# Early reads of the weight matrices, a new order of the first matmuls, and a finer last column in a fused GFNet plus gated-MLP kernel

## The chip, the cores and the metric

The kernel runs on one core of one Trainium2 chip. The metric is device time in microseconds (us), the median over several executions. In the text PE is the matmul engine, DVE is VectorE, ACT is ScalarE, POOL is GpSimd, and SP is SyncE, which issues most of the DMAs.

## The reference

x has 2048 rows of 512, in bf16. Three terms are added: x itself, a spectral filter of the normalised x, and a gated MLP of the normalised x.

```python
def reference(A_x, A_w_r, A_w_i, B_x, B_w_gate, B_w_up, B_w_down):
    x = A_x                                   # (1, 2048, 512)
    xn = _layernorm(x, axis=-1)
    # spectral: rfft2(xn) * (w_r + 1j*w_i), then irfft2
    # gated MLP: g = xn @ w_gate, u = xn @ w_up   (512 x 1792)
    #            (gelu(g) * u) @ w_down           (1792 x 512)
    return x + _A_ref(xn, A_w_r, A_w_i) + _B_ref(xn, B_w_gate, B_w_up, B_w_down)
```

## The kernel before

The 2048 rows are 16 "columns" of 128 rows each. A column is loaded, its mean and variance are taken (`stats`, `mean`), it is normalised to `xn`, transposed to `xnT` (columns 0 to 3 on PE, the others by DMA), and multiplied by Wg and Wu into `g_ps` and `u_ps`. Then ACT makes the gelu `ge` and DVE the product `hT`. The spectral part (`bp`, `dp`, `ep`, `gp`, `yp`) is woven between these units. At the end `y_ps` = `hT` times `Wd_sb` is added to x and stored.

A small planner orders all of this. Each operation is entered with an engine, an expected duration, a priority `key`, a landing time `t_min` where it needs a DMA, and the rotating PSUM buffers it takes and gives back. The planner simulates the engines and fixes each engine's order. Nothing is reordered at run time: an engine whose next instruction is not ready simply waits.

```python
    load_x(0, 1)                                   # columns 0 and 1, then weights in thirds
    load_x(1, 1)
    for f0, f1 in ((0, 512), (512, 1024)):
        load_w(Wg_sb, f0, f1)
        load_w(Wu_sb, f0, f1)
        if f0 == 0:
            load_x(2, 2)
    load_x(4, 4)
    # ... the last third of the weights, the rest of x, RF (a DFT table), constants ...
    LAND = {0: 2.9, 1: 3.8, 2: 7.9, 3: 7.9}        # landing times that the planner believes
    WG_LAND = [5.6] * 4 + [9.3] * 4 + [15.0] * 6
    WU_LAND = [7.0] * 4 + [10.8] * 4 + [17.0] * 6
    # ... the index table idx_t, issued last of these ...

def unit(k, c0, n, f0, m=1):                       # n columns, m chunks of 128 features
    g = add("PE", occ, lambda: mm("g_ps", "G", Wg_sb), src, key=1000 + k, acq=("G",), t_min=WG_LAND[f0 + m - 1])
    u = add("PE", occ, lambda: mm("u_ps", "U", Wu_sb), src, key=1000.5 + k, acq=("U",), t_min=WU_LAND[f0 + m - 1])
    # ... ge on ACT, h on DVE ...

todo = [(0, 1, 0, 2), (0, 1, 2, 2), (1, 1, 0, 4), (0, 2, 4, 2), (0, 2, 6, 2)]   # and so on

def forward(cg, kv):                               # bp: first DFT step of four columns
    for q in range(4):
        m = pe(0.224, lambda q=q: mm(q), [f], 10 * cg + q, acq=("S",), ...)
        bs_ops.append(add("ACT", 0.5, lambda q=q: out(q), [m], key=10 + cg + 0.1 * q, rel=("S",)))   # Bs <- bp

def down(c):                                       # y of one column; the last column in two halves
    w = D if c < NC - 1 else D // 2
    for o in range(0, D, w):
        # ... 14 matmuls with Wd, one with RI, the add of x on DVE, the store ...
```

(Cuts are marked with `# ...`; arguments that the argument here does not touch are left out.)

Of the kernel before, what the change touches and what calls it, by code (L numbers as in the profile page):

```python
# [10 lines left out]
P = 128  # L11
# [190 lines left out]
def kernel(  # L202
# [50 lines left out]
    def load_x(c0, n, eng=nc.sync):  # L253
        eng.dma_start(out=x_t[:, c0:c0 + n, :], in_=x_v[:, c0:c0 + n, :])

    def load_w(a, b, eng=nc.sync):
        nc.sync.dma_start(out=Wg_sb[:, :, a:b], in_=wg_v[:, :, a:b])
        eng.dma_start(out=Wu_sb[:, :, a:b], in_=wu_v[:, :, a:b])
# [17 lines left out]

    pin = tc.keep_in_program_order
    pin(nc.scalar.activation(out=root[:], in_=eps_t[:], func=AF.Sqrt, bias=eps_t[:], scale=1.0))
    load_x(0, 1)
    load_x(1, 1)  # L280
    for f0, f1 in ((0, 512), (512, 1024)):
        load_w(Wg_sb, f0, f1)
        load_w(Wu_sb, f0, f1)
        if f0 == 0:
            load_x(2, 2)
    load_x(4, 4)
    load_w(Wg_sb, 1024, DF)
    load_w(Wu_sb, 1024, DF)
    load_x(8, 4)
    nc.sync.dma_start(out=RF_t[:], in_=rf_d.rearrange("p (c k) -> p c k", c=NC))  # L290
    load_x(12, 4)
    load_consts("F0", "M0")
    LAND = {0: 2.9, 1: 3.8, 2: 7.9, 3: 7.9}
    LAND.update({c: 12.6 if c < 8 else 18.5 if c < 12 else 21.5 for c in range(4, NC)})
    WG_LAND = [5.6] * 4 + [9.3] * 4 + [15.0] * 6
    WU_LAND = [7.0] * 4 + [10.8] * 4 + [17.0] * 6
    RF_LAND = 20.0

    idx_t = pc.tile([P, 3], I32, name="idx_t")
    nc.sync.dma_start(out=idx_t[:], in_=nc.inline_tensor(idx_np, name="spec_rows").ap())  # L300
    for T, w_in in ((TR, A_w_r), (TI, A_w_i)):
        rows = w_in.rearrange("(kb a h g) k -> h kb a (g k)", kb=NC, h=2, a=8)
        Tf = T.rearrange("p j k -> p (j k)")
# [76 lines left out]
    def first_two():  # L380
        o = {}

        def v(k, fn, occ, deps=(), lat=None, t_min=0.0):
            o[k] = add("DVE", occ, fn, [o[d] for d in deps], key=-2000 + len(o), lat=lat, t_min=t_min,
                       after=o.get("last"))
            o["last"] = o[k]

        def root_of(c):
            o["root", c] = add("ACT", 0.31, lambda: A.activation(
                out=rstd[:, c:c + 1], in_=mv[:, c, 1:2], func=AF.Sqrt, bias=eps_t[:], scale=1.0),  # L390
                [o["mean", c]], key=-2000 + c)

        def T(c, h):
            o["T", c, h] = add("PE", 0.12, lambda: f_T(c, 2 * h, 2), [o["xn", c, h]], key=-2000 + 2 * c + h,
                               lat=0.36, acq=("S",))

        def recip(c):
            v(("rstd", c), lambda: V.reciprocal(out=rstd[:, c:c + 1], in_=rstd[:, c:c + 1]), 0.15, [("root", c)])

        def xn_(c, h):  # L400
            v(("xn", c, h), lambda: f_norm_v(c, 256 * h, 256), 0.27, [("rstd", c)], lat=0.4)

        def copy(c, h):
            v(("copy", c, h), lambda: f_Tc(c, 2 * h, 2), 0.25, [("T", c, h)], lat=0.4)
            o["copy", c, h].rel = ("S",)

        def stats(c):
            v(("stats", c), lambda: f_stats(c), 0.6, t_min=LAND[c], lat=0.7)

        def mean(c):  # L410
            v(("mean", c), lambda: f_mean(c), 0.1, [("stats", c)])
            root_of(c)

        stats(0)
        mean(0)
        stats(1)
        mean(1)
        recip(0)
        xn_(0, 0)
        xn_(0, 1)  # L420
        recip(1)
        table = add("ACT", 1.3, lambda: None, [o["root", 1]], key=-1500, lat=1.3)
        T(0, 0)
        T(0, 1)
        add("PE", 0.65, spin_on, [o["T", 0, 1]], key=-1500, lat=0.65, after=o["T", 0, 1])
        copy(0, 0)
        copy(0, 1)
        v("xn1", lambda: f_norm_v(1, 0, D), 0.33, [("rstd", 1)], lat=0.45)
        t = add("PE", 0.23, lambda: f_T(1, 0, NE), [o["xn1"]], key=-1998, lat=0.45, acq=("S",))
        xT_op[0], xn_op[0] = o["copy", 0, 1], o["xn", 0, 1]  # L430
        xT_op[1] = add("ACT", 0.5, lambda: f_Tc(1, 0, NE, A.copy), [t, table], key=-1200, rel=("S",))
        xn_op[1] = o["xn1"]
# [3 lines left out]
    def moments(c, key):  # L436
        s = add("DVE", 0.6, lambda: f_stats(c), key=key, t_min=LAND[c] if c < 4 else max(LAND[c], 14.7))
        return add("DVE", 0.1, lambda: f_mean(c), [s], key=key - 0.5)

    def second_two():  # L440
        m = [moments(c, -1200 + c) for c in (2, 3)]
        steps = rsqrt_steps(V, 2, 2)
        m = [add("DVE", 1.5, lambda: [f() for f in steps], m, key=-1190)]
        for c in (2, 3):
            xn_op[c] = add("DVE", 0.33, lambda c=c: f_norm_v(c, 0, D), m, key=-1180 + c, lat=0.53)
            t = add("PE", 0.23, lambda c=c: f_T(c, 0, NE), [xn_op[c]], key=-880 + c, lat=0.5, acq=("S",))
            e, f = ("ACT", A.copy) if c == 2 else ("DVE", V.tensor_copy)
            xT_op[c] = add(e, 0.5, lambda c=c, f=f: f_Tc(c, 0, NE, f), [t], key=-1100 + c, rel=("S",))
# [27 lines left out]
    def unit(k, c0, n, f0, m=1):  # L476
        sb, o, w = c0 // 4, (c0 % 4) * P, n * P
        alloc = None
        if sb < 3 and f0 == 0 and c0 % 4 == 0:
            def alloc():  # L480
                t = pc.tile([P, NFC, 512], BF16, name=f"hT{sb}", tag=("hT0", "hT1", "xn")[sb])
                hT.update({(sb, f): (t, f) for f in range(NFC)})
        elif sb == 3 and f0 % 4 == 0:
            def alloc():
                h = min(4, NFC - f0)
                t = pc.tile([P, h, 512], BF16, name=f"hT3{f0}", tag=("xnT0", "xnT1", "xnT2", "hT3")[f0 // 4])
                hT.update({(sb, f0 + f): (t, f) for f in range(h)})
        b = {}
        rhs = xnT[sb][:, :, c0 % 4:c0 % 4 + n, :].rearrange("p e c q -> p e (c q)")

        def mm(name, tag, W_):
            b[name] = ps.tile([P, m, w], F32, name=name, tag=tag, bufs=2)
            for f in range(m):
                for e in range(NE):
                    T_.matmul(b[name][:, f], lhsT=W_[:, e, (f0 + f) * P:(f0 + f + 1) * P], rhs=rhs[:, e, :],  # L495
                              start=(e == 0), stop=(e == NE - 1))

        def f_ge():
            b["ge"] = pw.tile([P, m, w], BF16, name="ge", bufs=3)
            A.activation(out=b["ge"][:], in_=b["g_ps"][:], func=AF.Gelu_apprx_tanh)  # L500

        def f_h():
            if alloc:
                alloc()
            V.tensor_tensor(out=hT_of(sb, f0, m, o, w), in0=b["u_ps"][:], in1=b["ge"][:], op=ALU.mult)  # L505

        occ = m * {1: 0.228, 2: 0.437, 4: 0.863}[n]
        src = [xT_op[c] for c in range(c0, c0 + n)]
        g = add("PE", occ, lambda: mm("g_ps", "G", Wg_sb), src, key=1000 + k, lat=occ + 0.3, acq=("G",),
                t_min=WG_LAND[f0 + m - 1])  # L510
        u = add("PE", occ, lambda: mm("u_ps", "U", Wu_sb), src, key=1000.5 + k, lat=occ + 0.3, acq=("U",),
                t_min=WU_LAND[f0 + m - 1])
        ge = add("ACT", {1: 0.28, 2: 0.36, 4: 0.5}[n * m], f_ge, [g], key=-1000 + k,
                 lat={1: 0.38, 2: 0.48, 4: 0.7}[n * m], acq=("ge",), rel=("G",))
        h = add("DVE", {1: 0.21, 2: 0.34, 4: 0.61}[n * m], f_h, [ge, u], key=-1000 + k, rel=("U", "ge"))
        for c in range(c0, c0 + n):
            for f in range(f0, f0 + m):
                h_op[c, f] = h

    todo = [(0, 1, 0, 2), (0, 1, 2, 2), (1, 1, 0, 4), (0, 2, 4, 2), (0, 2, 6, 2)]  # L520
    todo += [(2, 2, f, 2) for f in range(0, 8, 2)]
    todo += [(0, 4, f) for f in range(8, NFC)]
    todo += [(4 * sb, 4, f) for sb in range(1, NSB) for f in range(NFC)]
# [269 lines left out]
    def down(c):  # L793
# [20 lines left out]
            nc.sync.dma_start(out=out_v[:, c, o:o + w], in_=b["y"][:, o:o + w])  # L814

        x = add("SP", 0.36, load, key=1000 + c, lat=2.6, acq=("y_sb",), t_min=100.0)
        w = D if c < NC - 1 else D // 2
        for o in range(0, D, w):
            k = 2000 + 10 * c + o / D
            m = add("PE", 14 * w * 0.000421, lambda o=o: mm(o, w), [h_op[c, f] for f in range(NFC)] + [wd],  # L820
                    key=k, acq=("S",))
            r = add("PE", w * 0.000421, lambda o=o: ri_mm(o, w), [m, yt_op[c], ri], key=k + 0.1,
                    lat=w * 0.000421 + 0.3)
            m.lat = m.occ
            t = add("DVE", 0.1 + w * 0.001, lambda o=o: total(o, w), [r, x], key=k, rel=("S",))
            add("SP", 0.36, lambda o=o: store(o, w), [t], key=k, lat=2.0, rel=("y_sb",) if o + w == D else ())

    for c in range(NC):
        down(c)
# [35 lines left out]
```

## Time and profile before

| | before |
|---|---|
| median, four runs | 180.45 us (180.31 to 180.52) |
| span in the profile | 178.5 us |
| PE dense from | about 10.3 us |
| end of the last matmul | 175.13 us |

The first lines are from the page of the kernel before: the span, the busy time and share of each engine with its instruction count (PEld is PE's weight load, which overlaps PE), and the shares of the chain of waits that ended last.

```profile
span 178.5 us, 3086 instructions
...
PE 172.8 (97%) x1100; PEld 95.7 (54%) x1118; DVE 117.0 (66%) x261; ACT 95.9 (54%) x172; POOL 19.6 (11%) x60
...
PE 90%; DMA 4%; ACT 2%; SPq 1%; issue 1%; DVE 1%
...
```

PE is busy 97% of the span, so there seems to be nothing left. The Trainium skill (Perfetto Trace Analysis, "Identifying the Most-Contended Engine") warns that the matmul busy share is a poor measure of headroom. Part of the busy time here is filler (`spin` matmuls that keep PE running while data arrives), so the start has to be read in time.

The timeline of the kernel before, cut to the lines that matter: start in us, duration, engine, source line, operation, output<-inputs, shape, count, and in brackets the idle time before it and what ended it. A merged line's duration includes the modelled end of the last matmul, so read the starts. SPq is SP issuing a DMA.

```profile
1.71 0.43 SPq L275 DMA_DIRECT2D Wg_sb<-in_B_w_gate_dram  x1
...
6.78 0.61 PE L495 MATMUL g_ps<-xnT,Wg_sb 128*128 128x128 bf16 x8
...
8.10 1.07 PE L495 MATMUL u_ps<-xnT,Wu_sb 128*128 128x128 bf16 x16
...
8.76 1.29 DVE L333 BATCH_NORM_STATS2 stats<-x_t 128x6 f32<-128x512 bf16 x2 [2.04 <-DMA x_t<-in_A_x_dram]
...
9.00 1.06 PE L495 MATMUL g_ps<-xnT,Wg_sb 128*128 128x128 bf16 x16
...
10.27 1.05 PE L495 MATMUL g_ps<-xnT,Wg_sb 128*128 128x256 bf16 x8 [0.21 <-DMA Wg_sb<-in_B_w_gate_dram]
...
11.15 1.06 PE L495 MATMUL u_ps<-xnT,Wu_sb 128*128 128x128 bf16 x16
...
22.14 1.03 PE L495 MATMUL g_ps<-xnT,Wg_sb 128*128 128x512 bf16 x3
...
```

Read it from the starts. The first eight g matmuls of column 0 start at 6.78. The u matmuls start at 8.10, when the first piece of Wu lands. Sixteen g matmuls of column 1 start at 9.00 and, at 54 ns each, are done near 9.87. Then PE stands for 0.4 us until 10.27, because its next instruction needs the second piece of Wg. At 11.15 follow sixteen u matmuls of column 1 whose data had been there by 9.0 (Wu from 8.1, column 1's `xnT` at the latest with the g matmuls of 9.00): they could have filled that gap. From 10.27 on PE never waits until well past 22.14, where the wide (512-column) units begin. That start at 22.14 is a good milestone: it holds everything that happened before it.

A table of windows of the same kernel, here for the DMA rate (the last number, in GB/s):

```profile
core 0: us, PE busy (x) PEld busy (x) DVE busy (x) ACT busy (x) POOL busy (x), PEclk, DMA share, GB/s
3.00:3.50 0.50, 0.50 (x5) 0.31 (x3) 0.50 (x1) 0.00 (x0) 0.00 (x0) 1.00 0.47 47
3.50:4.00 0.50, 0.50 (x2) 0.15 (x1) 0.34 (x2) 0.09 (x1) 0.00 (x0) 1.00 0.83 205
4.00:4.50 0.50, 0.50 (x3) 0.21 (x2) 0.48 (x1) 0.20 (x1) 0.00 (x0) 1.00 0.86 285
```

Between 3 and 4 us the DMA engines move little (47, then 205 GB/s). Column 0 of x has landed (its stats start at 2.96), column 1 lands by 4.02, and the first of the weights is only starting. Later the rate is near 390.

Two more places in the PE timeline of the kernel before, near 40 us and at the first dp matmul:

```profile
39.47 1.42 PE L565 MATMUL bp<-RF_t,xf 128*128 128x128 bf16 x16
...
40.73 1.03 PE L495 MATMUL g_ps<-xnT,Wg_sb 128*128 128x512 bf16 x4
...
55.43 0.61 PE L623 MATMUL dp<-CT,Bs 128*128 128x128 bf16 x8
```

Sixteen bp matmuls normally take 0.89 us from start to the next start; here it is 40.73 - 39.47 = 1.26, so 0.37 us are lost. The end of the timeline:

```profile
174.86 0.27 PE L808 MATMUL y_ps<-yt,RI_t 128*128 128x256 bf16 x1
175.17 0.42 DVE L811 TENSOR_TENSOR y_sb<-y_ps,y_sb 128x256 bf16<-128x256 f32 x1 [0.73 <-PE y_ps L808]
```

After that add the last store is issued; its landing takes 1.6 us, and the span ends at 178.5.

### The profile page before, as it was taken

The numbers are of one execution on the slowest core, as the hardware profiler recorded it, in microseconds if no ns is written. First come the engines' busy times: TensorE is split into PE (matmuls) and PEld (weight loads), VectorE is DVE, ScalarE is ACT, GpSimd is POOL, SyncE is SP. The second block draws the span as 40 slices with busy tenths as digits, with TensorE's granted clock in tenths as the row PEclk, the third lists the DMA queues.
The fourth block names the chain that finished last, engine by engine and source line by source line (L and its number), as shares of the span: only waits on it lengthen the run. The fifth ranks groups of instructions, "written<-read, shape, count | busy, mean of one in ns | idle before, by whom it ended". The sixth has DMA issues, their size and how long they took to land.

```text
span 178.5 us, 3086 instructions
## 1 busy us (share of the span) xinstructions
PE 172.8 (97%) x1100; PEld 95.7 (54%) x1118; DVE 117.0 (66%) x261; ACT 95.9 (54%) x172; POOL 19.6 (11%) x60
## 2 busy tenths in 40 slices
PE   7999999999999999999999999999999999999992
PEld 5688845464455544555555454454454445445461
DVE  3498999983843599979899999643616425334341
ACT  4633487969675988898899964362112112111200
POOL 1000363620576000000000000000000000000000
PEclk9999999999999999999999999999999999999999
DMA  4999944333392662211201520200122212222211
GB/s 117 350 384 393 371 130 95 79 63 32 70 296 106 217 200 59 56 26 37 54 23 44 130 69 15 59 0 0 62 88 88 90 59 62 90 87 63 84 33 59
DMA packets 21008, 19.36 MB, mean 108 GB/s; under 512 B 8128, under 2 KB 19520, under 8 KB 20992
## 3 DMA queue, kind: packets, MB, share of 16 engines
q1 hardware_dynamic: 20576, 17.84, 33.9%
q0 software_dynamic: 416, 1.32, 2.3%
q8 instruction: 9, 0.15, 0.3%
q14 instruction: 7, 0.06, 0.1%
HBM read 13.38 MB, written 2.10 MB: 87 GB/s over the span
## 4 chain that ended last, share of the span: by engine, by line
PE 90%; DMA 4%; ACT 2%; SPq 1%; issue 1%; DVE 1%
PE y_ps L804 27%; PE u_ps L495 26%; PE g_ps L495 25%; DMA Wg_sb<-in_B_w_gate_dram 4%; PE yp L756 2%; PE gp L726 2%; PE dp L623 2%; PE y_ps L808 2%; PE ep L632 2%; PE bp L565 1%; ACT Bs L535 1%; SPq L271 1%; ACT ge L500 1%; SPq L275 1%; DVE hT L505 0%
## 5 line engine op out<-in xcount | busy, mean ns | idle before, releaser
L495 PE MATMUL g_ps<-xnT,Wg_sb 128*128 128x512 bf16 (+2 forms) x268 | 57.1, 341 | 0.5 <-DMA Wg_sb<-in_B_w_gate_dram 0.2
L495 PE MATMUL u_ps<-xnT,Wu_sb 128*128 128x512 bf16 (+2 forms) x264 | 56.4, 340 | 0.3
L505 DVE TENSOR_TENSOR hT<-u_ps,ge 128x512 bf16<-128x512 f32 (+1 forms) x57 | 38.6, 678 | 19.3 <-PE u_ps L495 12.3
L804 PE MATMUL y_ps<-Wd_sb,hT 128*128 128x512 bf16 (+1 forms) x232 | 50.5, 366 | 0.3
L500 ACT ACTIVATE ge<-g_ps 128x512 bf16<-128x512 f32 (+1 forms) x57 | 34.1, 598 | 24.4 <-PE g_ps L495 23.0
L495 PEld LDWEIGHTS <-Wg_sb 128*128 128x128 bf16 x272 | 24.9, 98 | 21.5 <-DMA Wg_sb<-in_B_w_gate_dram 0.4
L495 PEld LDWEIGHTS <-Wu_sb 128*128 128x128 bf16 x272 | 24.8, 98 | 20.7 <-DMA Wu_sb<-in_B_w_up_dram 0.2
L804 PEld LDWEIGHTS <-hT 128*128 128x128 bf16 x238 | 22.9, 98 | 22.6
L762 ACT CAST yf<-yp 128x512 bf16<-128x512 f32 x16 | 9.3, 586 | 40.5 <-PE yp L756 40.5
L811 DVE TENSOR_TENSOR y_sb<-y_ps,y_sb 128x512 bf16<-128x512 f32 (+1 forms) x17 | 11.0, 659 | 30.2 <-PE y_ps L808 30.2
L637 ACT CAST E<-ep 64x512 bf16<-64x512 f32 x32 | 18.5, 578 | 0.9 <-PE ep L632 0.5
L333 DVE BATCH_NORM_STATS2 stats<-x_t 128x6 f32<-128x512 bf16 x16 | 10.4, 677 | 4.2 <-DMA x_t<-in_A_x_dram 4.0
L458 ACT ACTIVATE xn<-x_t,nb,rstd 128x512 bf16<-128x512 bf16 x12 | 9.8, 834 | 2.8 <-POOL nb L373 2.8
L535 ACT CAST ds<-dp 128x512 bf16<-128x512 f32 x16 | 9.2, 597 | 0.6 <-PE dp L623 0.5
L535 ACT CAST Gs<-gp 128x512 bf16<-128x512 f32 x16 | 8.7, 591 | 0.6 <-PE gp L726 0.5
L535 ACT CAST Bs<-bp 128x512 bf16<-128x512 f32 x16 | 8.5, 611 | 0.0
L768 DVE TENSOR_TENSOR lv<-yf 128x512 bf16<-128x512 bf16 x16 | 6.1, 421 | 1.5 <-ACT yf L762 0.7
L756 PEld LDWEIGHTS <-Gs 128*128 128x128 bf16 x64 | 4.8, 98 | 3.5
L775 DVE TENSOR_TENSOR yt<-lv 128x512 bf16<-128x512 bf16 x16 | 6.1, 421 | 0.3
L756 PE MATMUL yp<-CT,Gs 128*128 128x128 bf16 x64 | 6.0, 219 | 0.1
L808 PE MATMUL y_ps<-yt,RI_t 128*128 128x512 bf16 (+1 forms) x17 | 5.9, 366 | 0.0
L632 PE MATMUL ep<-ds,CT 128*128 128x512 bf16 x16 | 5.9, 379 | 0.0
(72 smaller groups left out, 121.5 us busy)
## 6 DMA issues: line engine op xcount, KB each, us to landing
F<-F SPq DMA_DIRECT2D x32, 64.0 KB, 2.0
y_sb<-in_A_x_dram SPq DMA_DIRECT2D x16, 128.0 KB, 2.1
out_dram<-y_sb SPq DMA_DIRECT2D x15, 128.0 KB, 1.7
Wd_sb<-in_B_w_down_dram SPq DMA_DIRECT2D x1, 1792.0 KB, 7.6
x_t<-in_A_x_dram SPq DMA_DIRECT2D x3, 512.0 KB, 11.5
Wg_sb<-in_B_w_gate_dram SPq DMA_DIRECT2D x2, 512.0 KB, 5.9
Wu_sb<-in_B_w_up_dram SPq DMA_DIRECT2D x2, 512.0 KB, 6.9
Wg_sb<-in_B_w_gate_dram SPq DMA_DIRECT2D x1, 768.0 KB, 9.4
```

The costliest lines, as they stand in the source:

```text
L333: V.bn_stats(out=st[:], in_=x_t[:, c, :])
L458: xn_op[c] = add("ACT", 0.72, lambda c=c: A.activation(out=xn[:, c, :], in_=x_t[:, c, :], func=AF.Identity, bias=nb[:, c:c + 1], scale=rst ...
L495: T_.matmul(b[name][:, f], lhsT=W_[:, e, (f0 + f) * P:(f0 + f + 1) * P], rhs=rhs[:, e, :], start=(e == 0), stop=(e == NE - 1))
L500: A.activation(out=b["ge"][:], in_=b["g_ps"][:], func=AF.Gelu_apprx_tanh)
L505: V.tensor_tensor(out=hT_of(sb, f0, m, o, w), in0=b["u_ps"][:], in1=b["ge"][:], op=ALU.mult)
L535: A.copy(out=o, in_=i)
L632: T_.matmul(t[:], lhsT=cc("L" if g + h else "L0"), rhs=b["ds", h][:], start=True, stop=True)
L637: A.copy(out=b["E"][64 * h:64 * h + 64, r], in_=b["ep", h][64 * r:64 * r + 64])
L756: T_.matmul(t[:, q], lhsT=late["G"][:, q, c0 + j], rhs=IQ[q], start=(q == 0), stop=(q == 3), skip_group_check=True)
L804: T_.matmul(b[o][:], lhsT=hT_of(sb, f, 1, cl * P, P)[:, 0], rhs=Wd_sb[:, f, o:o + w], start=(f == 0), stop=False)
L808: T_.matmul(b[o][:], lhsT=late["RI"][:, c, :], rhs=late["yt"][:, c, o:o + w], start=False, stop=True)
L811: V.tensor_tensor(out=b["y"][:, o:o + w], in0=b[o][:], in1=b["y"][:, o:o + w], op=ALU.add)
```

## The change

The intent: read one element of every fourth row of both weight matrices before anything else, so that a first touch of these matrices would not hold up the real loads; put the small index table ahead of the weights; split some loads; correct the landing times in the plan; order the first units so that no engine waits; and cut the last column finer so that the tail is shorter.

```diff
+    ahead = pc.tile([P, 2], BF16, name="ahead")
+    for k, w in enumerate((B_w_gate, B_w_up)):
+        nc.scalar.dma_start(out=ahead[:, k:k + 1], in_=w.rearrange("(i e) f -> i e f", e=NE)[:, 0, 0:1])
     load_x(0, 1)
     load_x(1, 1)
+    idx_t = pc.tile([P, 3], I32, name="idx_t")
+    nc.sync.dma_start(out=idx_t[:], in_=nc.inline_tensor(idx_np, name="spec_rows").ap())
 # ... weights in the same order; x columns 4 to 11 in pairs, RF in two halves ...
-    LAND = {0: 2.9, 1: 3.8, 2: 7.9, 3: 7.9}
+    LAND = {0: 2.9, 1: 3.5, 2: 8.8, 3: 8.8}
-    WG_LAND = [5.6] * 4 + [9.3] * 4 + [15.0] * 6
-    WU_LAND = [7.0] * 4 + [10.8] * 4 + [17.0] * 6
+    WG_LAND = [6.6] * 4 + [10.2] * 4 + [15.0] * 6
+    WU_LAND = [8.0] * 4 + [11.7] * 4 + [17.0] * 6
 # ... column 1's mean behind the first half of column 0's xn ...
 # ... h of the first two units held back behind the steps of columns 2 and 3 ...
-    todo = [(0, 1, 0, 2), (0, 1, 2, 2), (1, 1, 0, 4), (0, 2, 4, 2), (0, 2, 6, 2)]
+    todo = [(0, 1, 0, 4), (1, 1, 0, 4), (0, 2, 4, 2), (0, 2, 6, 2)]
 # ... g of unit 0 and u of unit 2 may be split into smaller pieces of PE work ...
-        w = D if c < NC - 1 else D // 2
-        for o in range(0, D, w):
+        for o, w in ((0, D),) if c < NC - 1 else ((0, 256), (256, 128), (384, 128)):
```

In the order that results, PE does column 1's sixteen u matmuls before the second piece of Wg instead of after it.

More of the change, by code (lines that the diff above doesn't have):

```diff
@@ L278 @@
     pin(nc.scalar.activation(out=root[:], in_=eps_t[:], func=AF.Sqrt, bias=eps_t[:], scale=1.0))
+    ahead = pc.tile([P, 2], BF16, name="ahead")
+    for k, w in enumerate((B_w_gate, B_w_up)):
+        nc.scalar.dma_start(out=ahead[:, k:k + 1], in_=w.rearrange("(i e) f -> i e f", e=NE)[:, 0, 0:1])
     load_x(0, 1)
     load_x(1, 1)
-    for f0, f1 in ((0, 512), (512, 1024)):
-        load_w(Wg_sb, f0, f1)
-        load_w(Wu_sb, f0, f1)
-        if f0 == 0:
-            load_x(2, 2)
-    load_x(4, 4)
+    idx_t = pc.tile([P, 3], I32, name="idx_t")
+    nc.sync.dma_start(out=idx_t[:], in_=nc.inline_tensor(idx_np, name="spec_rows").ap())
+    load_w(Wg_sb, 0, 512)
+    load_w(Wu_sb, 0, 512)
+    load_x(2, 2)
+    load_w(Wg_sb, 512, 1024)
+    load_w(Wu_sb, 512, 1024)
+    load_x(4, 2)
+    load_x(6, 2)
     load_w(Wg_sb, 1024, DF)
     load_w(Wu_sb, 1024, DF)
-    load_x(8, 4)
-    nc.sync.dma_start(out=RF_t[:], in_=rf_d.rearrange("p (c k) -> p c k", c=NC))
+    load_x(8, 2)
+    load_x(10, 2)
+    for c in range(0, NC, 8):
+        nc.sync.dma_start(out=RF_t[:, c:c + 8], in_=rf_d.rearrange("p (c k) -> p c k", c=NC)[:, c:c + 8])
     load_x(12, 4)
     load_consts("F0", "M0")
-    LAND = {0: 2.9, 1: 3.8, 2: 7.9, 3: 7.9}
+    LAND = {0: 2.9, 1: 3.5, 2: 8.8, 3: 8.8}
     LAND.update({c: 12.6 if c < 8 else 18.5 if c < 12 else 21.5 for c in range(4, NC)})
-    WG_LAND = [5.6] * 4 + [9.3] * 4 + [15.0] * 6
-    WU_LAND = [7.0] * 4 + [10.8] * 4 + [17.0] * 6
+    WG_LAND = [6.6] * 4 + [10.2] * 4 + [15.0] * 6
+    WU_LAND = [8.0] * 4 + [11.7] * 4 + [17.0] * 6
     RF_LAND = 20.0
-    idx_t = pc.tile([P, 3], I32, name="idx_t")
-    nc.sync.dma_start(out=idx_t[:], in_=nc.inline_tensor(idx_np, name="spec_rows").ap())
     for T, w_in in ((TR, A_w_r), (TI, A_w_i)):
@@ L416, in first_two @@
         stats(1)
-        mean(1)
         recip(0)
         xn_(0, 0)
+        mean(1)
         xn_(0, 1)
-        recip(1)
         table = add("ACT", 1.3, lambda: None, [o["root", 1]], key=-1500, lat=1.3)
@@ L427, in first_two @@
         copy(0, 1)
+        recip(1)
         v("xn1", lambda: f_norm_v(1, 0, D), 0.33, [("rstd", 1)], lat=0.45)
@@ L438, in moments @@
         return add("DVE", 0.1, lambda: f_mean(c), [s], key=key - 0.5)
+    hold = {}
     def second_two():
@@ L443, in second_two @@
         m = [add("DVE", 1.5, lambda: [f() for f in steps], m, key=-1190)]
+        hold[0] = m[0]
         for c in (2, 3):
             xn_op[c] = add("DVE", 0.33, lambda c=c: f_norm_v(c, 0, D), m, key=-1180 + c, lat=0.53)
+            hold[1] = xn_op[c]
             t = add("PE", 0.23, lambda c=c: f_T(c, 0, NE), [xn_op[c]], key=-880 + c, lat=0.5, acq=("S",))
@@ L489, in unit, with mm @@
         rhs = xnT[sb][:, :, c0 % 4:c0 % 4 + n, :].rearrange("p e c q -> p e (c q)")
-        def mm(name, tag, W_):
-            b[name] = ps.tile([P, m, w], F32, name=name, tag=tag, bufs=2)
-            for f in range(m):
+        def mm(name, tag, W_, fs=range(m)):
+            if fs[0] == 0:
+                b[name] = ps.tile([P, m, w], F32, name=name, tag=tag, bufs=2)
+            for f in fs:
                 for e in range(NE):
@@ L508, in unit, with split @@
         src = [xT_op[c] for c in range(c0, c0 + n)]
-        g = add("PE", occ, lambda: mm("g_ps", "G", Wg_sb), src, key=1000 + k, lat=occ + 0.3, acq=("G",),
-                t_min=WG_LAND[f0 + m - 1])
-        u = add("PE", occ, lambda: mm("u_ps", "U", Wu_sb), src, key=1000.5 + k, lat=occ + 0.3, acq=("U",),
-                t_min=WU_LAND[f0 + m - 1])
+        def split(name, tag, W_, key, t, h):
+            o = None
+            for f in range(0, m, h):
+                o = add("PE", occ * h / m, lambda f=f: mm(name, tag, W_, range(f, f + h)), [o] if f else src, key=key,
+                        lat=occ * h / m + 0.3, acq=() if f else (tag,), t_min=t[f0 + f + h - 1])
+            return o
+        g = split("g_ps", "G", Wg_sb, 1000 + k, WG_LAND, 2 if k == 0 else m)
+        u = split("u_ps", "U", Wu_sb, 1000.5 + k, WU_LAND, 1 if k == 2 else m)
         ge = add("ACT", {1: 0.28, 2: 0.36, 4: 0.5}[n * m], f_ge, [g], key=-1000 + k,
                  lat={1: 0.38, 2: 0.48, 4: 0.7}[n * m], acq=("ge",), rel=("G",))
-        h = add("DVE", {1: 0.21, 2: 0.34, 4: 0.61}[n * m], f_h, [ge, u], key=-1000 + k, rel=("U", "ge"))
+        h = add("DVE", {1: 0.21, 2: 0.34, 4: 0.61}[n * m], f_h, [ge, u], key=-1000 + k, rel=("U", "ge"),
+                after=hold.get(k))
         for c in range(c0, c0 + n):
@@ L816, in down @@
         x = add("SP", 0.36, load, key=1000 + c, lat=2.6, acq=("y_sb",), t_min=100.0)
-        w = D if c < NC - 1 else D // 2
-        for o in range(0, D, w):
+        for o, w in ((0, D),) if c < NC - 1 else ((0, 256), (256, 128), (384, 128)):
             k = 2000 + 10 * c + o / D
-            m = add("PE", 14 * w * 0.000421, lambda o=o: mm(o, w), [h_op[c, f] for f in range(NFC)] + [wd],
+            m = add("PE", 14 * w * 0.000421, lambda o=o, w=w: mm(o, w), [h_op[c, f] for f in range(NFC)] + [wd],
                     key=k, acq=("S",))
-            r = add("PE", w * 0.000421, lambda o=o: ri_mm(o, w), [m, yt_op[c], ri], key=k + 0.1,
+            r = add("PE", w * 0.000421, lambda o=o, w=w: ri_mm(o, w), [m, yt_op[c], ri], key=k + 0.1,
                     lat=w * 0.000421 + 0.3)
             m.lat = m.occ
-            t = add("DVE", 0.1 + w * 0.001, lambda o=o: total(o, w), [r, x], key=k, rel=("S",))
-            add("SP", 0.36, lambda o=o: store(o, w), [t], key=k, lat=2.0, rel=("y_sb",) if o + w == D else ())
+            t = add("DVE", 0.1 + w * 0.001, lambda o=o, w=w: total(o, w), [r, x], key=k, rel=("S",))
+            add("SP", 0.36, lambda o=o, w=w: store(o, w), [t], key=k, lat=2.0, rel=("y_sb",) if o + w == D else ())
     for c in range(NC):
```

## The prediction

> **What bounds it.** The chain of waits is 90% PE. In a table of windows PE is busy 9.70 of 9.70 us between 10.3 and 20 us, and 19.8 to 19.9 of every 20 us after; the granted clock is full. So the time is: the time until PE is dense (about 10.3 us), then fixed matmul work to 175.1 us, then a tail. Only those first and last stretches can give anything.
>
> Start, from the timeline and the landings: x column 0 lands at 2.95, column 1 at 4.0, the first quarters of Wg at 6.6 and Wu at 8.1, x columns 2,3 at 8.7, Wg's second piece at 10.2, Wu's at 11.65. Real matmuls begin at 6.7. Between 6.7 and 10.3 PE does 48 matmuls of 128 columns (54 ns each) and four transposes, and stands about 0.23 us for Wu and 0.4 us for Wg's second piece. The DMA rate is near 390 GB/s, but 49, 45 and 143 GB/s from 3.0 to 3.75 us, when Wg is first read, and 260 to 285 from 7 to 8 us, when Wu is first read: about 0.5 and 0.3 us of transfer lost (estimate from those rates).
>
> **What changes.**
> 1. Two 128-element reads touch both matrices ahead. The first is issued before the activation table load; the second only after the first square root, about 2.9 us (estimate: 0.45 us per issue, 1.28 table load, 0.29 activation). If first touch is the cost, Wg's 0.5 us and Wu's 0.3 us shrink. The Trainium skill (DMA: Bandwidth & Descriptors, "Issuing engines are not separate DMA queues") says transfers from both engines interleave on the same 16 DMA engines, so the touches also take time beside x; no trace yet shows how much.
> 2. The index table ahead of weights costs one issue, 0.33 us, before Wg's. The queue is backlogged: 0 to 0.3 us of landing.
> 3. Order on PE: column 1's 16 u matmuls come before Wg's second piece instead of after, filling the 0.4 us wait. PE order is otherwise the same until the transposes of columns 2,3. These now come four u matmuls after 16 g matmuls; by my sum (Wu landing + 4.8 us = 12.85) PE is then 0.3 us early for xn of column 3, which VectorE finishes at 13.1 as before. Of 0.53 us won, 0.15 to 0.2 is handed back: net 0.35 to 0.4 with landings unchanged.
> 4. mean(1) behind the first xn half: 0.1 us earlier, hidden behind Wu's landing.
> 5. Last column 256+128+128: PE work equal (54 against 109 ns). The last add goes from 0.42 to about 0.28 us (estimate: 0.69 at 512, 0.42 at 256 columns), the last matmul's end 0.05 earlier; the store about equal. Net 0.15 to 0.2 us.
> 6. Split x and RF loads, recounted landings: reorder the middle, where PE is dense; within 0.15 us.
>
> **Sum.** 0.4 (start) + 0.2 (tail) + 0.2 (touches, half believed, less the index issue) = 0.8 us of 180.4. Predicted 179.6 us, 179.0 to 180.15 in 8 of 10. Faster by over 2%: 1%; within 2%: 98%; slower: 1%.
>
> **Signs.** Right: PE's wait for Wg's second piece gone; PE dense from about 8.1 us but for a short wait before column 3's transposes; last add near 0.28 us; the rate dip at 3.0 to 3.75 us shallower, Wg and Wu landing up to 0.5 us earlier. Wrong: x column 0 lands later than 3.0; Wg or Wu later than before; a dip unchanged; new gaps on PE in the middle.
>
> **What would break it.** Touches delaying column 0 or the weights by over 0.5 us; or Wu landing at 7.3 and x columns 2,3 with it, which gives about 1.3 us in all.

## The result, and the profile after

The changed kernel took 179.46 us (median of four, 179.13 to 179.74); the kernel before 180.45 us. The ratio is 0.9945, with a 95% interval of 0.9925 to 0.9965. Ratios are quoted for fast runs of the same rounds; they are not the ratio of the medians, and for the experiments the plain means of all listed runs differ from them by up to 0.0005. Two later sets of rounds with the unaltered changed kernel gave 0.9963 and 0.9961.

The page of the changed kernel (its profile fell on its fastest run, 179.13 us):

```profile
span 177.4 us, 3118 instructions
...
PE 172.0 (97%) x1115; PEld 95.8 (54%) x1133; DVE 116.7 (66%) x261; ACT 96.6 (54%) x171; POOL 20.1 (11%) x60
...
PE 83%; ACT 5%; DMA 3%; issue 3%; POOL 2%; DVE 1%; SPq 1%; ACTq 0%
...
```

The timeline of its start, with the lines that answer to those of before. ACTq is ACT issuing a DMA.

```profile
0.80 0.40 ACTq L281 DMA_DIRECT2D ahead<-in_B_w_gate_dram  x1
...
1.28 0.40 ACTq L281 DMA_DIRECT2D ahead<-in_B_w_up_dram  x1
...
1.71 0.42 SPq L285 DMA_DIRECT2D idx_t<-spec_rows  x1
2.18 0.43 SPq L275 DMA_DIRECT2D Wg_sb<-in_B_w_gate_dram  x1
...
6.29 0.62 PE L506 MATMUL g_ps<-xnT,Wg_sb 128*128 128x128 bf16 x8
...
7.73 1.07 PE L506 MATMUL u_ps<-xnT,Wu_sb 128*128 128x128 bf16 x16 [0.15 <-DMA Wu_sb<-in_B_w_up_dram]
...
8.41 1.29 DVE L339 BATCH_NORM_STATS2 stats<-x_t 128x6 f32<-128x512 bf16 x2 [1.89 <-DMA x_t<-in_A_x_dram]
...
8.64 1.06 PE L506 MATMUL g_ps<-xnT,Wg_sb 128*128 128x128 bf16 x16
...
9.53 1.06 PE L506 MATMUL u_ps<-xnT,Wu_sb 128*128 128x128 bf16 x16
...
10.42 1.91 PE L506 MATMUL g_ps<-xnT,Wg_sb 128*128 128x256 bf16 x16
...
12.03 0.72 DVE L345 TENSOR_SCALAR xn<-x_t,mv,rstd 128x512 bf16<-128x512 bf16 x2
...
12.61 0.61 PE L351 MATMUL tp<-ident_t,xn 128*128 128x128 bf16 x8
...
```

The 0.4 us stand before the second piece of Wg is gone: g at 8.64, u at 9.53, and the 256-column g at 10.42, each following the last without a gap. From the first g matmuls to the milestone PE waits once, for Wu at 7.73. My feared wait before the transposes of columns 2 and 3 is below 0.1 us, because columns 2 and 3 arrived at 8.41 here, not at 8.76.

The DMA rate in the same windows of the changed kernel:

```profile
3.00:3.50 0.50, 0.50 (x5) 0.31 (x3) 0.47 (x1) 0.00 (x0) 0.00 (x0) 1.00 0.51 41
3.50:4.00 0.50, 0.50 (x2) 0.15 (x1) 0.47 (x3) 0.02 (x1) 0.00 (x0) 1.00 0.62 63
4.00:4.50 0.50, 0.50 (x3) 0.21 (x2) 0.50 (x2) 0.28 (x1) 0.00 (x0) 1.00 0.75 217
```

The dip is not shallower. It is 0.5 us longer: 63 and 217 GB/s where before had 205 and 285.

The timeline from the wide units to the first dp matmul, changed kernel (PE, and near 40 us the steps of ACT that bear on it):

```profile
21.35 1.03 PE L506 MATMUL g_ps<-xnT,Wg_sb 128*128 128x512 bf16 x3
...
36.35 0.81 ACT L468 ACTIVATE xn<-x_t,nb,rstd 128x512 bf16<-128x512 bf16 x1 [0.92 <-POOL nb L379]
...
38.25 1.54 ACT L552 CAST Bs<-bp 128x512 bf16<-128x512 f32 x3
...
39.54 0.83 PE L582 MATMUL bp<-RF_t,xf 128*128 128x128 bf16 x12
...
40.16 0.61 ACT L552 CAST Bs<-bp 128x512 bf16<-128x512 f32 x1
...
40.82 0.38 PE L582 MATMUL bp<-RF_t,xf 128*128 128x128 bf16 x4 [0.45 <-ACT Bs L552]
...
41.04 1.03 PE L506 MATMUL u_ps<-xnT,Wu_sb 128*128 128x512 bf16 x4
...
54.89 0.61 PE L640 MATMUL dp<-CT,Bs 128*128 128x128 bf16 x8
```

The milestone moved from 22.14 to 21.35, by 0.79 us. But the stretch from there to the first dp matmul grew from 55.43 - 22.14 = 33.29 to 54.89 - 21.35 = 33.54 us. PE's third bp group now loses 41.04 - 39.54 - 0.89 = 0.61 us, waiting for ACT to copy the group before out of PSUM. That hands 0.24 us back. ACT itself is late here: at 36.35 it had stood 0.92 us for `nb`, a bias that POOL computes; three of the four copies then took 0.51 us each, as planned, and the last 0.61. The tail:

```profile
174.41 0.22 PE L825 MATMUL y_ps<-yt,RI_t 128*128 128x128 bf16 x1
174.66 0.29 DVE L828 TENSOR_TENSOR y_sb<-y_ps,y_sb 128x128 bf16<-128x128 f32 x1 [0.55 <-PE y_ps L825]
```

The last add takes 0.29 us instead of 0.42, the last store lands in 1.5 us instead of 1.6 (the view has one decimal), and from the end of the last matmul to the end of the span it is 177.4 - 174.63 = 2.77 us instead of 3.37.

### The profile page after: what moved, and what is told of

The parts are those of the page before. It is cut to its first block, busy times and chain, and to the rows that moved or that the text cites. A ratio compares the mean times of both kernels' runs of the same rounds, so it can differ in the third digit from the quotient of the medians.

```text
span 177.4 us, 3118 instructions
## 1 busy us (share of the span) xinstructions
PE 172.0 (97%) x1115; PEld 95.8 (54%) x1133; DVE 116.7 (66%) x261; ACT 96.6 (54%) x171; POOL 20.1 (11%) x60
## 4 chain that ended last, share of the span: by engine, by line
PE 83%; ACT 5%; DMA 3%; issue 3%; POOL 2%; DVE 1%; SPq 1%; ACTq 0%
PE y_ps L821 27%; PE u_ps L506 23%; PE g_ps L506 22%; DMA Wu_sb<-in_B_w_up_dram 3%; PE dp L640 2%; ACT Bs L552 2%; PE yp L773 2%; PE gp L743 2%; PE y_ps L825 2%; PE ep L649 2%; ACT xn L468 2%; ACT ge L511 1%; DVE hT L516 1%; PE bp L582 1%; POOL t L367 0%
## 5 line engine op out<-in xcount | busy, mean ns | idle before, releaser
L506 PE MATMUL g_ps<-xnT,Wg_sb 128*128 128x512 bf16 (+2 forms) x265 | 56.4, 340 | 0.4
L516 DVE TENSOR_TENSOR hT<-u_ps,ge 128x512 bf16<-128x512 f32 x56 | 38.6, 688 | 19.1 <-PE u_ps L506 10.5
L821 PE MATMUL y_ps<-Wd_sb,hT 128*128 128x512 bf16 (+2 forms) x246 | 50.6, 355 | 0.3
L511 ACT ACTIVATE ge<-g_ps 128x512 bf16<-128x512 f32 x56 | 33.9, 606 | 21.4 <-PE g_ps L506 17.6
L828 DVE TENSOR_TENSOR y_sb<-y_ps,y_sb 128x512 bf16<-128x512 f32 (+2 forms) x18 | 11.1, 631 | 30.0 <-PE y_ps L825 30.0
L825 PE MATMUL y_ps<-yt,RI_t 128*128 128x512 bf16 (+2 forms) x18 | 6.1, 355 | 0.0
L743 PEld LDWEIGHTS <-F 128*128 128x128 bf16 x64 | 4.5, 98 | 2.6
```

The costliest lines, as they stand in the source:

```text
L506: T_.matmul(b[name][:, f], lhsT=W_[:, e, (f0 + f) * P:(f0 + f + 1) * P], rhs=rhs[:, e, :], start=(e == 0), stop=(e == NE - 1))
L511: A.activation(out=b["ge"][:], in_=b["g_ps"][:], func=AF.Gelu_apprx_tanh)
L516: V.tensor_tensor(out=hT_of(sb, f0, m, o, w), in0=b["u_ps"][:], in1=b["ge"][:], op=ALU.mult)
L821: T_.matmul(b[o][:], lhsT=hT_of(sb, f, 1, cl * P, P)[:, 0], rhs=Wd_sb[:, f, o:o + w], start=(f == 0), stop=False)
L825: T_.matmul(b[o][:], lhsT=late["RI"][:, c, :], rhs=late["yt"][:, c, o:o + w], start=False, stop=True)
L828: V.tensor_tensor(out=b["y"][:, o:o + w], in0=b[o][:], in1=b["y"][:, o:o + w], op=ALU.add)
```

## The experiments

All kernels gave correct results. Each set of rounds shares runs of the kernel before on the same chip. Five rounds each. I first show the runs, then one table of milestones over all profiles, because a single profile of the start turned out to scatter.

### The changed kernel again

No edit.

> The changed kernel unaltered, to have its spread and a second profile on the chip of the next three. Same result as on record: 0.7 to 1.3 us under the kernel before. The first profile showed the wide 512-column units 0.79 us earlier (21.35 against 22.14), then 0.25 us given back at a wait for the evacuation of bp near 40 us, then 0.6 us in the tail of which the shorter add and store explain 0.25. If the other 0.35 us of the tail is chance, this profile's tail (end of the last add to end of span) is not again 0.4 us shorter than before's; if it belongs to the 128-column store, it is.

Measured: 179.72 us (179.51 to 180.0), ratio to before 0.9963 (0.995 to 0.9976). The tail in the profile was 2.83 us, short again. The milestone was at 21.82, so 0.47 us of the first profile's 0.79 were luck with landings.

### Without the touches

```diff
-    ahead = pc.tile([P, 2], BF16, name="ahead")
-    for k, w in enumerate((B_w_gate, B_w_up)):
-        nc.scalar.dma_start(out=ahead[:, k:k + 1], in_=w.rearrange("(i e) f -> i e f", e=NE)[:, 0, 0:1])
```

> The changed kernel without the two reads of one element per row; nothing else moves, the plan is the same. Theory A (first touch of the matrices is what the touches hide): Wg lands at 6.5 to 6.9 and Wu at 8.0 to 8.4 us instead of 6.25 and 7.7, PE starts the u matmuls 0.3 us later or more, and the time is 0.3 to 0.5 us above the changed kernel's. Theory B (the touches do nothing, or cost as much as they bring, and the earlier landing comes from the order of loads): Wg and Wu land within 0.1 us of the changed kernel or earlier, time within 0.15 us of it or below.

Measured: 179.28 us (179.09 to 179.69), ratio 0.9941 (0.9928 to 0.9954), so below the changed kernel of the same rounds by 0.44 us in the medians, 0.36 in the means. The windows of this kernel:

```profile
3.00:3.50 0.50, 0.50 (x5) 0.31 (x3) 0.45 (x1) 0.00 (x0) 0.00 (x0) 1.00 0.61 50
3.50:4.00 0.50, 0.50 (x2) 0.15 (x1) 0.47 (x3) 0.00 (x1) 0.00 (x0) 1.00 0.74 74
4.00:4.50 0.50, 0.50 (x3) 0.21 (x2) 0.50 (x2) 0.29 (x1) 0.00 (x0) 1.00 0.71 201
```

The dip between 3 and 4.5 us is the same without touches (50, 74, 201 against 41, 63, 217). Theory A, that the touches hide a first touch, is refuted. Wu's first use was at 7.84 (7.73, 7.99 and 8.27 in the three profiles of the changed kernel), as in theory B. Removing them did not merely leave the time alone; in these rounds it improved it, though the two intervals still touch (0.9954 against 0.995).

### The index table back in its old place

```diff
     load_x(1, 1)
-    idx_t = pc.tile([P, 3], I32, name="idx_t")
-    nc.sync.dma_start(out=idx_t[:], in_=nc.inline_tensor(idx_np, name="spec_rows").ap())
 # ...
     RF_LAND = 20.0
+    idx_t = pc.tile([P, 3], I32, name="idx_t")
+    nc.sync.dma_start(out=idx_t[:], in_=nc.inline_tensor(idx_np, name="spec_rows").ap())
```

> The changed kernel with the index table back behind the constants, where the kernel before has it. Theory C (the early index load only costs an issue and stirs 128 twelve-byte packets into the first weights): Wg and Wu land 0.1 to 0.4 us earlier than in the changed kernel and the time falls by 0.1 to 0.4 us. Theory D (the queue is backlogged, one issue ahead costs nothing; or the delay of Wg's issue even gives the touches time to land): landings and time within 0.1 us, or later.

Measured: 179.28 us (179.21 to 179.74), ratio 0.9937 (0.9924 to 0.995): again 0.44 us below the changed kernel. Wg was issued at 1.71 instead of 2.18, and u started at 7.57. Theory C holds for the time (0.44 us, a little over its 0.4) and for u. This run and the one without touches are compared with the same five runs of the changed kernel, so a chance in those would show in both; the last rounds repeat only the two edits together. In its profile, columns 2 and 3 came late (9.05) and took the gain of that one execution away.

### The last column in two halves again

```diff
-        for o, w in ((0, D),) if c < NC - 1 else ((0, 256), (256, 128), (384, 128)):
+        for o, w in ((0, D),) if c < NC - 1 else ((0, 256), (256, 256)):
```

> The changed kernel with the last column in 256+256 again. If the split is worth only the shorter add and store seen in the profiles, time is 0.2 to 0.3 us above the changed kernel's; if the whole 0.6 us of the first profile's tail is its work, 0.5 to 0.7 us above. PE's last matmul ends at the same time within 0.1 us in both cases.

Measured: 180.0 us (179.47 to 180.19), ratio 0.9969 (0.9956 to 0.9982): 0.28 us above the changed kernel in the medians, 0.19 in the means. The intervals overlap, so the runs alone don't settle the size. With its tail as in the kernel before, this kernel is still faster than it (the interval ends at 0.9982): that part of the gain lies before the tail. The tail in its profile was 3.06 us.

### The old load list under the new order

```diff
-    ahead = pc.tile([P, 2], BF16, name="ahead")
 # ... the loop of touches, and the early index table, go too ...
-    load_x(4, 2)
-    load_x(6, 2)
+    load_x(4, 4)
-    load_x(8, 2)
-    load_x(10, 2)
-    for c in range(0, NC, 8):
-        nc.sync.dma_start(out=RF_t[:, c:c + 8], in_=rf_d.rearrange("p (c k) -> p c k", c=NC)[:, c:c + 8])
+    load_x(8, 4)
+    nc.sync.dma_start(out=RF_t[:], in_=rf_d.rearrange("p (c k) -> p c k", c=NC))
 # ... index table behind the constants, as in the kernel before ...
```

> The changed kernel with the load list of the kernel before: no touches, index table late, x columns 4 to 11 and RF unsplit; its order of work on PE and VectorE, its recounted landings and its last column stay. Theory P (the gain is the order of work on PE in the first 13 us plus the tail): the time is 0.8 to 1.2 us under the kernel before, as good as the changed kernel or better, and PE shows no wait for Wg's second piece. Theory L (the gain is the loads): within 0.4 us of the kernel before.

Measured: 179.59 us (179.28 to 180.2) against 180.25, ratio 0.9967 (0.9952 to 0.9982). The fall is 0.66 us in the medians, 0.71 in the means: a little less than I expected of theory P, and more than the 0.4 us that theory L allows. So the order and the tail carry most of the gain; the new load list as a whole adds nothing that shows (the changed kernel had ratios of 0.9945, 0.9963 and 0.9961). PE shows no wait for Wg's second piece.

### The touches alone, on the kernel before

```diff
+    ahead = pc.tile([P, 2], BF16, name="ahead")
+    for k, w in enumerate((B_w_gate, B_w_up)):
+        nc.scalar.dma_start(out=ahead[:, k:k + 1], in_=w.rearrange("(i e) f -> i e f", e=NE)[:, 0, 0:1])
     load_x(0, 1)
     load_x(1, 1)
```

> The kernel before with the two touches put first, nothing else. If first touch is the cost that they hide, Wg lands 0.3 us or more earlier than 6.6 us and Wu than 8.1, and the time falls by 0.3 to 0.5 us. If they do nothing, landings stay within the spread of 0.4 us seen between profiles of one start, the dip in the DMA rate between 3 and 4 us stays, and the time is within 0.2 us of the kernel before, or up to 0.4 above if they cost as in the run without them.

Measured: 180.6 us (180.25 to 181.2), ratio 1.0009 (0.9996 to 1.0022). No gain; a loss is not clear of noise. Its profile fell on the slowest run, 181.2 us. Wu was used earlier there (7.76 against 8.10), but the 256-column g began at 10.40, when the second piece of Wg landed, no earlier than before. The dip stayed (111 and 150 GB/s from 3 to 4 us). The bp group near 40 us lost 0.79 us instead of 0.37; ACT had stood 2.25 us for POOL's `nb` there, 1.66 in the kernel before.

### Neither touches nor early index

Both of the edits above together.

> The changed kernel with neither touches nor the early index load; x and RF split as in it. Each undone alone gave 0.44 us against the changed kernel of the same rounds. If these are two separate costs, 0.6 to 0.9 us under the changed kernel (178.8 to 179.1 where before is 180.45); if they are one cost or largely scatter, 0.3 to 0.5 us under it (179.2 to 179.4).

Measured: 179.17 us (179.05 to 179.62), ratio 0.9943 (0.993 to 0.9955). The last runs repeat it beside the changed kernel. This is what undoing either of the two gave, not the double. So the two costs don't add.

One more comparison lies in these rounds. This kernel and the one with the old load list differ only in the split of x columns 4 to 11 and RF, and this one is 0.42 us faster in the medians, 0.40 in the means (the intervals touch: 0.993 to 0.9955 against 0.9952 to 0.9982). The last rounds point the same way: the kernel with only the new order is 0.70 us in the means behind the one without early reads, and the tail explains only 0.19 to 0.28 of that. So the split loads may bring what the early reads cost. Where, the profiles don't show: the milestones are 21.35 with the split and 21.24 without.

### Column 1 of x issued from ACT's queue

```diff
-    load_x(1, 1)
+    load_x(1, 1, nc.scalar)
```

on the kernel without touches and early index.

> As the last kernel, but the load of x column 1 is issued by ACT at 0.8 us beside that of column 0 on SP, so that Wg's issue starts at about 1.25 us instead of 1.7. Theory I (the dip at 3 to 4 us is the time from Wg's issue to its first bytes, about 1.9 us from issue to full rate, which the 256 KB of x are too short to cover): the dip starts at the same time and shrinks by 0.3 us or more, Wg and Wu land 0.3 us earlier, time 0.2 to 0.4 us below the last kernel. Theory F (it is a first touch of the matrix, whatever its issue): the dip is as long as before, only its start may move.

Measured: 180.14 us (179.61 to 180.79), ratio 0.9998 (0.9979 to 1.0017): 0.97 us worse than the run it was made from. The windows of this kernel:

```profile
3.00:3.50 0.50, 0.37 (x4) 0.21 (x2) 0.00 (x0) 0.00 (x0) 0.00 (x0) 1.00 0.74 119
3.50:4.00 0.50, 0.09 (x1) 0.09 (x1) 0.11 (x1) 0.00 (x0) 0.00 (x0) 1.00 0.92 307
4.00:4.50 0.50, 0.50 (x2) 0.17 (x2) 0.50 (x1) 0.00 (x0) 0.00 (x0) 1.00 1.08 377
```

Wg was issued at 1.24 us, and the rate was 307 by 3.5 to 4.0 us, where the run without it (Wg issued at 1.71) had 217 and the changed kernel (2.18) had 63. So the dip's end follows the issue of Wg, about 2 us behind it: theory I for the dip. Its start stays near 3.0 us in all three (over 200 GB/s from 2.75 to 3, at most 111 from 3 to 3.25), so the dip is shorter and not only moved, as theory F would have it. But column 0 landed at 3.89 instead of 3.31 (2.96 to 3.42 in all other profiles), and the first g matmuls started at 7.10 instead of 6.40. The Trainium skill (DMA: Bandwidth & Descriptors, "Issuing engines are not separate DMA queues") says that DMAs of all issuing engines run on the same 16 engines and interleave, and that a second issuer only saves issue time. This run agrees: it saved 0.47 us of issue, and paid 0.58 us of column 0's landing. My expectation of a gain had left this out. Whether column 1 beside it or the earlier start of Wg delayed column 0 is not separated. The profile, on one of the faster runs (179.69 us), shows 0.48 us of loss at the milestone; what the slower runs lost beyond that is not shown.

### The changed kernel, and the one without early reads, in the same rounds

> The changed kernel once more, as the base of these rounds. 0.7 to 1.0 us under the kernel before; the first wide g unit starts between 21.3 and 22.1 us, and from there to the first dp matmul it takes 33.5 us, as in every profile of this plan, against 33.29 in the kernel before.

> Neither touches nor the early index load, in the same rounds as the changed kernel. If these two cost time, as three pairs of runs suggest, 0.3 to 0.6 us under the changed kernel; if those were scatter of chips and rounds, within 0.15 us of it.

Measured: the changed kernel 179.64 us (179.16 to 179.8), without touches and early index 179.26 us (178.94 to 179.7); ratios to before 0.9961 (0.9931 to 0.9991) and 0.9947 (0.9918 to 0.9977). That is 0.38 us in the medians, 0.32 in the means. On this chip the runs of the kernel before fell into two groups (179.5 to 179.9 and 180.4 to 180.9), so the intervals against before are wide.

### Only the new order

```diff
 # the old load list under the new order, and:
-        for o, w in ((0, D),) if c < NC - 1 else ((0, 256), (256, 128), (384, 128)):
+        for o, w in ((0, D),) if c < NC - 1 else ((0, 256), (256, 256)):
```

> The kernel before with only the new order of the first matmuls and VectorE steps and the recounted landings; load list and last column as before. By the profiles so far: start 0.8 to 0.9 us earlier (first wide g unit at 21.25 to 21.4 against 22.14), 0.24 us given back near 40 us, tail as before: 0.5 to 0.7 us under the kernel before. If the new order were worth less than the loads, under 0.3 us.

Measured: 179.99 us (179.79 to 180.11), ratio 0.9981 (0.9952 to 1.0009). That is 0.45 us in the medians and 0.26 in the means, below my 0.5 to 0.7. The milestone was at 21.80, later than I expected; the middle gave back 0.25; the tail was 3.37 as before. The start of this kernel:

```profile
7.08 0.61 PE L500 MATMUL g_ps<-xnT,Wg_sb 128*128 128x128 bf16 x8
...
8.20 1.06 PE L500 MATMUL u_ps<-xnT,Wu_sb 128*128 128x128 bf16 x16
```

The late u at 8.20 is not a late Wu: that landed near 7.6, 5.4 us after its issue, and PE's list of waits has no wait for it. The first g was late. Column 0 landed at 3.42 instead of 2.99 in the run with the old load list, and the six filler matmuls before g took 1.12 us from their start (5.96) to that of g, instead of 0.73; why they were slower is not shown. By itself this run does not show the order faster than before beyond its interval. With the finer last column (the old load list, above) the two together do.

### One planning number corrected

```diff
-            bs_ops.append(add("ACT", 0.5, lambda q=q: out(q), [m], key=10 + cg + 0.1 * q, rel=("S",)))
+            bs_ops.append(add("ACT", 0.6, lambda q=q: out(q), [m], key=10 + cg + 0.1 * q, rel=("S",)))
```

on the kernel without touches and early index.

> As the one without touches and early index, with one planning number changed: ACT's copy of bp counted at 0.6 us, as traces show it (0.51 to 0.61), not 0.5. The plan then puts the third group of bp matmuls one unit of 0.86 us later. If the 0.4 us wait of PE for the evacuation of bp is that misplanned order, the wait is gone, the stretch from the first wide g unit to the first dp matmul falls from 33.5 to 33.1 to 33.3 us and the time by 0.2 to 0.4 us against the run without this. If the wait only moves, the stretch stays at 33.5.

Measured: 178.6 us (178.3 to 178.8), ratio 0.9904 (0.9875 to 0.9933). That is the fastest kernel: 0.66 us below the run it was made from and about 1.0 below the changed kernel of the same rounds, with no overlap of its runs (at most 178.8) with either of them (at least 178.94 and 179.16). The PE timeline near 40 us in this kernel:

```profile
39.54 1.03 PE L503 MATMUL u_ps<-xnT,Wu_sb 128*128 128x512 bf16 x4
...
40.41 1.06 PE L579 MATMUL bp<-RF_t,xf 128*128 128x128 bf16 x16
...
41.30 1.03 PE L503 MATMUL g_ps<-xnT,Wg_sb 128*128 128x512 bf16 x4
```

The bp group comes one unit later and takes 41.30 - 40.41 = 0.89 us, without a wait. The stretch from the milestone to the first dp matmul fell to 32.93 us, 0.58 below the plan it came from and 0.36 below the kernel before, whose own 0.37 us wait is gone too. The fall is more than my 0.2 to 0.4, as the whole stall went (0.61 us), not the 0.4 that the list of waits names. ACT is hardly earlier here: it again stands 0.84 us for POOL's `nb`, and its last copy of the group before ends at 40.69, against 40.77 in the changed kernel. What the number changed is the order: PE has a u unit to do in the meantime.

### All profiles side by side

Start times in us: the first u matmul, the first stats of column 2, the milestone (first wide g), then the stretch to the first dp matmul, and the tail (span less the end of the last matmul; the span has one decimal).

| kernel | first u | stats col. 2 | milestone | to first dp | tail |
|---|---|---|---|---|---|
| before | 8.10 | 8.76 | 22.14 | 33.29 | 3.37 |
| before, touches | 7.76 | 8.68 | 22.27 | 34.33 | 3.20 |
| changed | 7.73 | 8.41 | 21.35 | 33.54 | 2.77 |
| changed, again | 7.99 | 8.88 | 21.82 | 33.52 | 2.83 |
| changed, third | 8.27 | 8.92 | 21.89 | 33.52 | 2.76 |
| last column in halves | 8.51 | 9.13 | 22.12 | 33.53 | 3.06 |
| no touches | 7.84 | 8.52 | 21.46 | 33.52 | 2.88 |
| index late | 7.57 | 9.05 | 21.99 | 33.52 | 2.75 |
| neither | 7.56 | 8.42 | 21.35 | 33.52 | 2.89 |
| neither, again | 7.48 | 8.07 | 21.08 | 33.51 | 2.87 |
| old load list | 7.57 | 8.31 | 21.24 | 33.53 | 3.09 |
| only the order | 8.20 | 8.39 | 21.80 | 33.54 | 3.37 |
| column 1 from ACT | 8.22 | 7.94 | 21.83 | 33.51 | 2.92 |
| planning number | 7.66 | 8.42 | 21.35 | 32.93 | 2.88 |

Three readings follow.

First, in each of the twelve profiles of the new order the milestone is, within 0.05 us, the later of two sums: first u + 13.60, and stats of column 2 + 12.93. The two constants are fitted to this table. (Changed, again: 21.59 and 21.81, measured 21.82. Neither, again: 21.08 and 21.00, measured 21.08.) So the start of the first u matmuls and the landing of columns 2 and 3 set the milestone. What sets the first u differs. In the five profiles with the index table early, the first u comes 1.37 to 1.50 us after the first g, and PE or its weight loads wait for Wu. In the seven with it late, it comes 1.12 to 1.18 us after, and the lists of waits name none for Wu: there the first g decides, and what decides that (column 0, Wg, the filler).

Second, the profiles suggest that the early reads make just these two later. The five profiles with the index table early have u at 8.07 on average, the six of the new order with it late and the usual x loads at 7.67; Wu is issued 0.47 us later in the five (2.65 against 2.18), and lands 5.0 to 5.8 us after its issue in the five, 5.2 to 5.4 in the six. The five with touches (new order) have columns 2 and 3 at 8.88, the six without (usual x loads) at 8.36. One profile alone is chance, and the two lists overlap a little in each case. The reading for the touches is the weaker one: four of those five also have the index table early, and in the old order, with one profile each, columns 2 and 3 are no later with touches (8.68 against 8.76). How 256 two-byte reads would delay columns 2 and 3 by half a microsecond is not shown.

Third, the middle is fixed by the plan to 0.03 us in the eleven profiles of the new order that share it, with the old load list too, so the split of the loads has no part in its loss. The tail falls from a mean of 3.25 us in four profiles with halves (3.06 to 3.37) to 2.86 in ten with quarters at the end (2.75 to 3.09).

## Why the prediction was right, and where not

The time was 179.6 predicted, 179.46 measured, inside the range. Point by point:

1. **What bounds it: right.** All of the gain came in the first 22 us and in the tail; what moved between them was a loss (point 7).
2. **Touches: wrong.** I counted half of a first-touch cost as saved, and with the index issue 0.2 us of gain. The runs show no gain: the dip is unchanged without them, and taking them out wins 0.36 us in the means of one set of rounds (ratio intervals 0.9928 to 0.9954 against 0.995 to 0.9976). The size is open: in its first rounds the changed kernel had 0.9945, which is also what the kernels with one or both taken out and the loads still split had (0.9937 to 0.9947). Both were issued before any weight, at 0.80 and 1.28 (I had put the second at 2.9), and landed 2.4 and 2.6 us later; whether still earlier ones would do more is not tested. The step that failed is reading a dip in the DMA rate at the first use of a matrix as a cost of first use. Moving Wg's issue by 0.47 us in either direction moves the dip's end by about as much; the two kernels with touches left in and out at equal issue times have the same dip.
3. **Index table ahead: sign right, size low.** I gave it 0 to 0.3 us. Undoing it wins 0.33 us in the means, on the same base as point 2, and the first u comes 0.4 us later with it. That the two undone together win no more than either alone is measured twice (0.32 us in the last rounds); why, stays open.
4. **Order on PE: right.** With the landings of before (u at 8.10, column 2 at 8.76), the two sums above give 21.70, so 0.44 us earlier than 22.14; I had said 0.35 to 0.4 net, with the same two landings as the new limits. The three profiles of the changed kernel range from 0.25 to 0.79, with later and earlier landings; the kernel before has one. The 0.4 us stand is gone in all of them. In time, the order alone gave 0.26 us in the means, not clear of noise, and with the tail 0.71, which is.
5. **mean(1) moved: hidden**, as said, in the changed kernel: in its three profiles PE, or its weight load, still waits for Wu after the first g matmuls. Without the early index the first g does count (first reading), and no run tests this edit by itself.
6. **Last column: too small.** Predicted 0.15 to 0.2. The one-edit comparison says 0.19 to 0.28, the profiles' tails 0.39 (3.25 to 2.86). The add is 0.13 shorter, the store at most 0.1; the remainder after landing is not explained.
7. **"Within 0.15 us" in the middle: wrong.** All eleven profiles of the new plan lose 0.22 to 0.25 us between the milestone and the first dp matmul. The third bp group follows the second too closely in the new plan, and meets a longer wait for ACT. The change of one planning number shows that this order is the cause: with the group one unit later the wait vanished and the time fell by 0.66 us, though ACT's copies ended only 0.08 us earlier. Why ACT is behind the plan is only partly shown: its copies took 0.51 to 0.61 us, but the larger piece just before is its stand of 0.92 us for POOL. (What the split of the loads is worth in the runs, perhaps 0.4 us, I had not counted at all.)

So the sum came out well by luck: its errors cancelled. Against the profile of the kernel before, the three profiles of the changed kernel average 0.45 us at the milestone (predicted 0.4 for the order and 0.2 for the loads), a loss of 0.24 in the middle (predicted none) and 0.58 in the tail (predicted 0.2), in all 0.8. Of my signs, the vanished wait for Wg and the shorter add came; so did three that I had called wrong: the dip unchanged, column 0 later than 3.0 us (3.03, 3.15, 3.19), and a longer wait in the middle.

## What to carry to other kernels

When engines run a fixed order, fill a wait with work whose data is already there before trying to bring data sooner: the reorder took the 0.4 us stand away in every profile, while the early reads brought nothing that shows. Check a static plan against the trace, also off the bottleneck: one group of matmuls put a unit too early, behind copies on ACT that ran late, cost PE 0.6 us, as much as I had hoped for from order and loads together. And before acting on a dip in a single profile, take several profiles of the same kernel: here the start alone scattered by 0.5 us.

## What the Trainium skill lacked or had wrong

- DMA: Bandwidth & Descriptors, "Specifications": the page gives 512 B as the least size for line rate. In the last store, 32 KB in 256-byte rows landed in 1.5 us, 64 KB in 512-byte rows in 1.5 to 1.6; 32 KB in longer rows were not measured. The page doesn't say what such rows do to the latency of one small store.
- The same page, "Issuing engines are not separate DMA queues": it says that spreading issues saves only issue time, not that it can cost. With column 1 issued from ACT beside column 0, and Wg's issue thereby 0.47 us earlier, column 0 landed 0.58 us later (3.31 to 3.89) in the profiles and the run was 0.97 us slower.
- No page that I found tells what a few hundred two-byte reads at the start cost the loads behind them. Here taking out 256 of them won 0.36 us in the means of one set of rounds; the profiles of the new order have columns 2 and 3 of x about 0.5 us later with them, partly together with another edit.
- Perfetto Trace Analysis, "Identifying Performance Opportunities": it does not say how far one kernel's start scatters between executions. Three profiles of the same kernel put the milestone at 21.35, 21.82 and 21.89 us.
